# A gated causal convolution on one core: the last octet's second gate, transposes and output projection in a finer order, and the second window's remainder loaded ahead of its x

## The chip, the cores and the metric

The kernel runs on one core of one Trainium2 chip. The metric is device time in microseconds (us), from one launch of the whole program. A time is a median over several runs; the profile is of one further execution, whose own time differs a little from the median.

## The reference

`x` is 2 x 16000 x 144, `w` 15 x 144 x 288, `w_o` 144 x 144, all bfloat16. A causal convolution in time with 15 taps, two steps apart, gives 288 channels. The first 144 go through tanh, the other 144 through a sigmoid, the product `z` is multiplied by `w_o`.

```python
dil = 2
pad = (K - 1) * dil
xp = jnp.pad(x, ((0, 0), (pad, 0), (0, 0)))
h = sum(einsum('btc,cd->btd', xp[:, pad - i*dil : pad - i*dil + T, :], w[i]) for i in range(K))
z = jnp.tanh(h[..., :D]) * sigmoid(h[..., D:])
return z @ w_o
```

(The loop over the taps is written as a sum here; D is 144, K 15, T 16000.)

## The kernel before

**Windows and octets.** Each batch's 16000 time steps are cut into 8 windows of 2048 (the last overlaps its neighbour), so there are NW = 16. Within a window, time is 16 m + r: m runs over the 128 partitions of a result, r over 16 residues. An octet is the 8 residues of one parity of one window, so there are NO = 32 octets, two to a window. An octet's result `y` is 128 x 8 x 288 in float32: 8 rows (residues) of 288 channels.

**The convolution.** `load` brings a window's first 128 channels in by a transposing DMA (`xn`, line 89), channels on partitions. Differences of shifted copies of it (`d2`, `d4`, `d8`, `d24`, ..., line 160, on VectorE, DVE below) feed a scheme that needs fewer matrix multiplications than taps times rows; all the convolution's matmuls are issued at line 302. Partial sums go from PSUM through ScalarE copies (ACT, lines 331, 335, 366) and DVE additions (lines 369, 387, 392); the last of these write the rows of `y`. Rows 0, 2, 4, 6 of `y` come from the leaf B, rows 1 and 5 from `yC2_0` and `yC2_1`, rows 3 and 7 from `yC3_0` and `yC3_1`, which are written last.

**The remainder.** The last 16 of the 144 channels take another way. `gather` loads them as `xt` (line 99: 104 x 22 runs of 16 values, 32 bytes each). ACT copies them in order of residue (`xs`, line 113), DVE takes differences (`xs`, line 117), `spread` writes both to DRAM (`xg`, line 123), and two more transposing DMAs read them back as `rx` and `re` (line 128). All of these but window 0's `xt` and spreads are issued from SyncE's queue (SP).

**The gate and the output.** For each octet `act` issues a tanh and a sigmoid (ACT, line 397) over four rows of `y`: `th0`, `sg0` for rows 0, 2, 4, 6 and `th1`, `sg1` for rows 1, 3, 5, 7. `mult` forms the product `z` (DVE, line 404). A transposing DMA turns `z` into `zt` (line 408), `outproj` multiplies by `w_o` in three groups of at most three rows (line 434), `project_out` copies each group from PSUM to the window's output tile `o` (line 424 on ACT, 426 on DVE), and `store` writes a window (line 450).

**The last octets.** Octet 31's `z` is laid out by row (`by_phase`): blocks 0 to 7 hold 128 channels of a row each, block 8 the 16 remaining channels of all rows. TensorE (PE) transposes it with an identity matrix (`z_by_pe`, line 418), four blocks to a PSUM bank, and `outproj` takes block 8 first (line 438, against `wo_bd`), then a block for each row (line 441, against `wo_m`). Octets 29, 30 and 31 have their output in `finish_early`, just before octet 31's second product, and `finish`, after it; the last store is issued in two parts, from SP and ACT.

**What sets the order.** Nothing is scheduled by the compiler: each engine runs its instructions in the order in which the program issues them. In the steady part that order is a hand-written list, `PLAN`, of names with the octet that they are early or late by; `first` is the order of the opening. `late2 = [(2, "xl")]` stands ahead of it, so that window 1's `xn` (octet 2 is its first) is issued right behind window 0's `rx` and `re`; window 1's `xt` follows from `PLAN`.

PSUM is in three pools: `ps_a` (2 banks, `bank(True)`), `ps_bc` (5 banks, `bank(False)`) and `ps_o` (1 bank). A new tile waits for the readers of the one whose bank it takes.

Of the kernel before, what the change touches and what calls it, by code (L numbers as in the profile page):

```python
# [8 lines left out]
BF16 = mybir.dt.bfloat16  # L9
# [17 lines left out]
def kernel(  # L27
# [146 lines left out]
    def bank(a):  # L174
        return ps_a.tile([P, 512], F32, name="a", tag="a") if a else ps_bc.tile([P, 512], F32, name="bc", tag="bc")
# [169 lines left out]
    class Octet:  # L345
# [45 lines left out]
            y = self.get(y_pool, "y", [P, 8, D2], F32)  # L391
            nc.vector.tensor_tensor(out=y[:, k + 4 * i, :], in0=self.t[q][:, i, :], in1=ts[i][:, 0:D2], op=op)  # L392

        def act(self, k, name, lo, func):
            t = act_pool.tile([P, 4, D], BF16, name=name)
            self.g[name, k] = t
            nc.scalar.activation(out=t[:], in_=self.t["y"][:, k::2, lo:lo + D], func=func)  # L397

        def mult(self, k, part):
            z = self.get(z_pool, "z", [P, 9, CM], BF16)  # L400
            o, lo, n = dict(a=(z[:, k:8:2, :], 0, CM), b=(z[:, 8, :].rearrange("p (r c) -> p r c", c=CR)[:, k::2, :], CM, CR),
                            z=(z[:].rearrange("p g c -> p (g c)").rearrange("p (r c) -> p r c", c=D)[:, k::2, :], 0, D))[part]
            th, sg = self.g["th", k], self.g["sg", k]
            nc.vector.tensor_tensor(out=o, in0=th[:, :, lo:lo + n], in1=sg[:, :, lo:lo + n], op=ALU.mult)  # L404

    def z_load(z):
        zt = zt_pool.tile([P, 9, P], BF16, name="zt")
# [3 lines left out]
    def z_by_pe(o, blocks, by):  # L411

        zt, z = o.get(zt_pool, "zt", [P, 9, P], BF16), o.t["z"]
        for i in range(0, len(blocks), 4):
            b = blocks[i:i + 4]
            ps = bank(True)[:].bitcast(BF16).rearrange("p (g m) -> p g m", m=256)
            for k, g in enumerate(b):
                nc.tensor.transpose(ps[:, k, 0:P], z[:, g, :], ident[:])
            copy_by(by, zt[:, b[0]:b[-1] + 1:2, :], ps[:, 0:len(b), 0:P])
        o.zt = zt  # L420

    def copy_by(by, o, a):
        if by == "ACT":
            nc.scalar.copy(out=o, in_=a)  # L424
        else:
            nc.vector.tensor_copy(out=o, in_=a)  # L426

    def outproj(o, g, end=False):
        r0, n = 3 * g, min(3, 8 - 3 * g)
        o.po[g] = bank(False) if end else ps_o.tile([P, 512], F32, name="po", tag="po")  # L430
        if not o.by_phase:
            for c in range(r0, r0 + n + 1):
                a, e = max(c - 1, r0), min(c + 1, r0 + n)
                nc.tensor.matmul(o.po[g][:, (a - r0) * D:(e - r0) * D], lhsT=o.zt[:, c, :],  # L434
                                 rhs=wo_z[:, c, a - c + 1:e - c + 1, :].rearrange("p r e -> p (r e)"), start=c == r0, stop=c == r0 + n,
                                 skip_group_check=True)
            return
        nc.tensor.matmul(o.po[g][:, 0:n * D], lhsT=o.zt[:, 8, :], rhs=wo_bd[:, r0:r0 + n, :].rearrange("p r e -> p (r e)"),  # L438
                         start=True, stop=False)
        for i in range(n):  # L440
            nc.tensor.matmul(o.po[g][:, i * D:(i + 1) * D], lhsT=o.zt[:, r0 + i, :], rhs=wo_m[:], start=False, stop=i == n - 1)  # L441

    def project_out(o, ob, g, by="ACT"):
        r0, n = 3 * g, min(3, 8 - 3 * g)
# [13 lines left out]
    def issue(n, name):  # L458
        wi, rho = octs[n]
        if name == "xl":  # L460
            sets[wi].update(load(wi))
            sets[wi].update(steps=derive_steps(sets[wi]))
            return
        s = sets[wi]
        if name in fetch:
            fetch[name](wi)
            return
        if name in s["steps"]:
            s["steps"][name]()
            return  # L470
        if n not in live:
            live[n] = Octet(s, rho)
            live[n].by_phase = n == NO - 1
        o = live[n]
        if name[0] in "vkpd" and name[1] in "ABCE":
            leaf = getattr(o, name[1:3] if name[1] == "A" else name[1] + "1")
            if name[0] == "v":
                leaf.common()
            elif name[0] == "k":
                leaf.copy()  # L480
            else:
                (leaf.private if name[0] == "p" else leaf.dup)(int(name[-1]))
        elif name[:2] == "t3":
            o.t3(int(name[-1]))
        elif name[:3] == "a1s":
            o.a1s(int(name[-1]))
        elif name[0] == "q":
            o.q(*((o.A2, "q2") if name[1] == "2" else (o.A3, "q3")), int(name[-1]),
                ALU.subtract if name[1] == "2" else ALU.add)
        elif name[0] in "BC":  # L490
            getattr(o, name[0:2])(int(name[-1]))
        elif name[0] == "y":
            leaf = {"B": o.B1, "C": o.C1, "E": o.E1}["E" if name[1:3] == "C3" else name[1]]
            ts, q = (leaf.other, "q3") if name[1:3] == "B3" else (leaf.ts, "t3" if name[1:3] == "C3" else "q2")
            k = (0 if name[1] == "B" else 1) + (2 if name[2] == "3" else 0)
            o.out_y(k, ts, q, ALU.subtract if name[1] == "B" else ALU.add, int(name[-1]))
        elif name[:2] == "th":
            o.act(int(name[2]), "th", 0, ACT.Tanh)
        elif name[:2] == "sg":
            o.act(int(name[2]), "sg", D, ACT.Sigmoid)  # L500
        elif name[0] == "m":
            for part in "ab" if o.by_phase else "z":
                o.mult(int(name[1]), part)
        elif name == "zt":
            o.zt = z_load(o.t["z"])
        elif name[0] == "g":
            outproj(o, int(name[1]))
        elif name[:2] == "po":
            project_out(o, window_out(n), int(name[2]))
        else:  # L510
            assert name == "ost"
            store(wi, nc.scalar)

    def window_out(n):
        wi = octs[n][0]
        if wi not in outs:
            outs[wi] = os_pool.tile([P, 16, D], BF16, name="o")
        return outs[wi]

    def finish_early():  # L520

        n = NO - 3
        for g in range(3):
            outproj(live[n], g, g > 0)
        for g, by in ((0, "DVE"), (1, "DVE"), (2, "ACT")):
            project_out(live[n], window_out(n), g, by)
        z_by_pe(live[NO - 1], [0, 2, 4, 6], "ACT")

    def finish():
        n = NO - 2  # L530
        store(NW - 2, nc.sync)
        for g in range(3):
            outproj(live[n], g, True)
        for g in (0, 1):
            project_out(live[n], window_out(n), g)
        z_by_pe(live[n + 1], [1, 3, 5, 7], "DVE")
        z_by_pe(live[n + 1], [8], "DVE")
        project_out(live[n], outs[NW - 1], 2, "DVE")
        for g in range(3):
            outproj(live[n + 1], g, True)  # L540
        for g, by in ((0, "ACT"), (1, "DVE"), (2, "ACT")):
            project_out(live[n + 1], outs[NW - 1], g, by)
        store(NW - 1, nc.sync, 0, P // 2)
        store(NW - 1, nc.scalar, P // 2)

# [1 line left out]
    even = set(pre0) | set(fetch) | {"xl"}  # L547
    outwards = {"g0", "g1", "g2", "po0", "po1", "po2", "ost"}
    at_wg = next((at, i) for i, (name, at) in enumerate(plan) if name == "wg")
    def weights_out():  # L550

        nc.gpsimd.memset(wo_z[:], 0.0)
        nc.gpsimd.memset(wo_bd[:], 0.0)
        held = const.tile([1, 1], BF16)
        nc.gpsimd.tensor_copy(out=held[:], in_=ev[0:1, 0, 0:1])
        for g in range(9):
            if g:
                nc.gpsimd.dma_start(out=wo_z[0:CR * g, g, 0, :], in_=w_o[D - CR * g:D, :])
            if g < 8:
                nc.gpsimd.dma_start(out=wo_z[CR * g:P, g, 1, :], in_=w_o[0:P - CR * g, :])  # L560
        nc.gpsimd.dma_start(out=wo_m[:], in_=w_o[0:CM, :])
        for g in range(NG):
            nc.gpsimd.dma_start(out=wo_bd[g * CR:(g + 1) * CR, g, :], in_=w_o[CM:D, :])

    def evs():
# [3 lines left out]
    first = ["vA1", "kA1", lambda: raw_sums(1, (0,)), lambda: keep(1), "pA1_0", "pA1_1", "a1s_0", "a1s_1", "vA2", "kA2", lambda: keep(2), "vB",  # L569
             "kB", "pA2_0", "q2_0", "pA2_1", "q2_1", "vA3", "kA3", "pB_0", "dB_0", "pB_1", "dB_1", lambda: pre0["d24"](slice(1, 2)), "pA3_0",  # L570
             "q3_0", "pA3_1", "B2_0", "q3_1", "B2_1", evs, "yB2_0", pre0["d248"]]
    late2 = [(2, "xl")]
    for n, name in late2:
        issue(n, name)
    for f in first:
# [3 lines left out]
                  (n + at, n > 1 and n + at < 0, i, n, name) for i, (name, at) in enumerate(plan) for n in range(NO)  # L579
                  if not (name in even and (n % 2 or n == 0) or name == "ost" and n % 2 == 0  # L580
                          or name in outwards and n >= NO - 3 or name == "zt" and n == NO - 1))
    gates = [(NO - 1, "m1")]
    for *_, n, name in todo:
        if (n, name) in done:
            continue
        if (n, name) in gates:
            gates.clear()
            finish_early()
        issue(n, name)
    finish()  # L590
# [1 line left out]
_INS = ['x', 'w', 'w_o']  # L592
_OUTS = [((2, 16000, 144), 'bfloat16')]
# [25 lines left out]
```

## Time and profile before

| | us |
|---|---|
| median of 3 runs | 332.19 (331.83 to 332.69) |
| profiled execution, its own time | 332.82 |
| its span, first to last instruction | 330.8 |
| PE busy | 321.4 (97%) |
| PE's weight loads busy | 303.1 (92%) |
| DVE busy | 293.5 (89%) |
| ACT busy | 242.0 (73%) |
| POOL busy | 26.3 (8%) |

The span is what lies between the first and the last instruction; the time of the execution holds some 2 us more. PE is busy nearly all through, with a mean granted clock of 0.999. The opening (to about 24 us) and the end (from about 321 us) are the stretches in which PE waits for others.

In the profile's rows a start and a duration are in us from the span's start. "xn<-in_x_dram" is a write of tile xn from the input. "[0.66 <-DVE y L392]" behind a row says that the engine had been idle for 0.66 us and that a write of y on DVE, line 392, ended it. SPq and ACTq are the times that the queues took to issue a DMA, not the transfers.

### The profile page before, as it was taken

The numbers are of one execution on the slowest core, as the hardware profiler recorded it, in microseconds if no ns is written. First come the engines' busy times: TensorE is split into PE (matmuls) and PEld (weight loads), VectorE is DVE, ScalarE is ACT, GpSimd is POOL, SyncE is SP. The second block draws the span as 40 slices with busy tenths as digits, with TensorE's granted clock in tenths as the row PEclk, the third lists the DMA queues.
The fourth block names the chain that finished last, engine by engine and source line by source line (L and its number), as shares of the span: only waits on it lengthen the run. The fifth ranks groups of instructions, "written<-read, shape, count | busy, mean of one in ns | idle before, by whom it ended". The sixth has DMA issues, their size and how long they took to land.

```text
span 330.8 us, 7432 instructions
## 1 busy us (share of the span) xinstructions
PE 321.4 (97%) x2657; PEld 303.1 (92%) x2657; DVE 293.5 (89%) x664; ACT 242.0 (73%) x571; POOL 26.3 (8%) x56
## 2 busy tenths in 40 slices
PE   8899999999999999999999999999999999999993
PEld 3589999999999999999999999999999999999982
DVE  2889999989999998999999899999989999998683
ACT  2737777777877777788777778877777787777763
POOL 5959100000000000000000000000000000000000
PEclk9999999999999999999999999999999999999999
DMA  8779897895949579594979769495986859594113
GB/s 173 160 139 157 155 210 138 151 185 100 206 109 204 151 130 222 77 213 102 175 181 169 157 119 187 109 209 137 145 208 119 171 112 189 154 143 132 38 36 129
DMA packets 194993, 49.64 MB, mean 150 GB/s; under 512 B 190487, under 2 KB 192896, under 8 KB 194957
## 3 DMA queue, kind: packets, MB, share of 16 engines
q1 hardware_dynamic: 188894, 40.07, 69.6%
q10 hardware_dynamic: 4799, 8.58, 7.0%
q0 software_dynamic: 1264, 0.53, 0.9%
q8 instruction: 20, 0.33, 0.4%
q14 instruction: 16, 0.13, 0.1%
HBM read 2.82 MB, written 11.40 MB: 43 GB/s over the span
## 4 chain that ended last, share of the span: by engine, by line
PE 90%; DMA 4%; SPq 2%; DVE 2%; issue 1%; POOL 1%; ACT 0%; DVEq 0%
PE bc L302 56%; PE a L302 25%; PE po L434 9%; DMA xn<-in_x_dram 2%; DMA xt<-in_x_dram 1%; SPq L128 1%; DMA xg<-zero 1%; SPq L89 1%; DVE d L160 0%; DVE o L426 0%; DVE y L392 0%; DVE z L404 0%; POOL xg L123 0%; PE bc L438 0%; PE bc L441 0%
## 5 line engine op out<-in xcount | busy, mean ns | idle before, releaser
L302 PEld LDWEIGHTS <-d 128*128 128x128 bf16 x1792 | 225.4, 145 | 7.8 <-issue 1.4
L302 PE MATMUL bc<-w_all,d 128*128 128x288 bf16 x832 | 140.0, 286 | 0.3 <-DVE t L387 0.3
L392 DVE TENSOR_TENSOR y<-q,bc 128x288 f32<-128x288 f32 x192 | 86.4, 450 | 7.6 <-PE bc L302 5.7
L331 ACT COPY bc<-bc 128x288 f32<-128x288 f32 x97 | 38.5, 397 | 30.1 <-PE bc L302 24.3
L369 DVE TENSOR_TENSOR q<-a1s,a 128x288 f32<-128x288 f32 x126 | 54.2, 451 | 1.5 <-PE a L302 0.8
L424 ACT CAST o<-po 128x432 bf16<-128x432 f32 (+1 forms) x87 | 41.7, 479 | 17.1 <-PE po L434 17.1
L160 DVE TENSOR_TENSOR d<-d 128x516 bf16<-128x516 bf16 (+3 forms) x65 | 52.2, 805 | 0.0
L302 PE MATMUL a<-sm,d 128*128 128x288 bf16 x252 | 50.2, 286 | 0.0
L331 ACT COPY a<-a 128x288 f32<-128x288 f32 x95 | 36.6, 386 | 13.6 <-PE a L302 10.6
L160 DVE TENSOR_TENSOR d<-xn 128x516 bf16<-128x516 bf16 (+2 forms) x48 | 41.1, 859 | 5.1 <-DMA xn<-in_x_dram 5.1
L397 ACT ACTIVATE th<-y 128x576 bf16<-128x576 f32 x64 | 43.9, 685 | 1.1 <-DVE y L392 1.1
L397 ACT ACTIVATE sg<-y 128x576 bf16<-128x576 f32 x64 | 43.7, 683 | 0.0
L434 PE MATMUL po<-wo_z,zt 128*128 128x144 bf16 (+1 forms) x323 | 43.4, 253 | 0.0
L302 PE MATMUL bc<-bc,d 128*128 128x288 bf16 x256 | 41.8, 286 | 0.0
L302 PE MATMUL bc<-wo_p,re 128*128 128x288 bf16 x128 | 36.6, 286 | 0.0
L302 PE MATMUL bc<-we_r,re 128*128 128x288 bf16 x128 | 36.6, 286 | 0.0
L387 DVE TENSOR_TENSOR t<-q,bc 128x288 f32<-128x288 f32 x64 | 28.8, 451 | 8.3 <-PE bc L302 8.3
L434 PEld LDWEIGHTS <-zt 128*128 128x128 bf16 x341 | 29.9, 98 | 4.1
L335 ACT COPY bc<-bc 128x288 f32<-128x288 f32 x64 | 25.0, 393 | 11.2 <-PE bc L302 7.0
L392 DVE TENSOR_TENSOR y<-t,bc 128x288 f32<-128x288 f32 x64 | 26.1, 450 | 5.9 <-PE bc L302 5.9
L404 DVE TENSOR_TENSOR z<-th,sg 128x576 bf16<-128x576 bf16 (+1 forms) x66 | 29.1, 443 | 0.0
L302 PEld LDWEIGHTS <-re 128*128 128x128 bf16 x256 | 28.8, 113 | 0.0
(79 smaller groups left out, 275.5 us busy)
## 6 DMA issues: line engine op xcount, KB each, us to landing
out_dram<-o ACTq DMA_DIRECT2D x13, 576.0 KB
xg<-xs SPq DMA_DIRECT2D x30, 65.0 KB
xt<-in_x_dram SPq DMA_DIRECT2D x13, 71.5 KB
w_all<-in_w_dram SPq DMA_DIRECT2D x3, 288.0 KB
out_dram<-o SPq DMA_DIRECT2D x1, 576.0 KB
zt<-z SPq DMA_TRANSPOSE x31
out_dram<-o ACTq DMA_DIRECT2D x1, 468.0 KB
out_dram<-o ACTq DMA_DIRECT2D x1, 288.0 KB
```

Of the source, the lines that this page charges most:

```text
L89: nc.sync.dma_start_transpose(out=xn[:, lo:WB], in_=src)
L160: nc.vector.tensor_tensor(out=o, in0=a, in1=b_, op=ALU.subtract)
L302: nc.tensor.matmul(ps[:, 0:D2], lhsT=l, rhs=r, start=start, stop=stop, skip_group_check=on)
L331: nc.scalar.copy(out=self.ts[1][:, 0:D2], in_=self.ts[0][:, 0:D2])
L335: nc.scalar.copy(out=self.other[i][:, 0:D2], in_=self.ts[i][:, 0:D2])
L369: nc.vector.tensor_tensor(out=self.get(cp_pool, name, [P, 2, D2], F32)[:, i, :], in0=self.t["a1s"][:, i, :], in1=leaf.ts[i][:, 0:D2], op=op)
L387: nc.vector.tensor_tensor(out=self.get(cp_pool, "t3", [P, 2, D2], F32)[:, i, :], in0=self.t["q3"][:, i, :], in1=self.C1.ts[i][:, 0:D2], op ...
L392: nc.vector.tensor_tensor(out=y[:, k + 4 * i, :], in0=self.t[q][:, i, :], in1=ts[i][:, 0:D2], op=op)
L397: nc.scalar.activation(out=t[:], in_=self.t["y"][:, k::2, lo:lo + D], func=func)
L404: nc.vector.tensor_tensor(out=o, in0=th[:, :, lo:lo + n], in1=sg[:, :, lo:lo + n], op=ALU.mult)
L424: nc.scalar.copy(out=o, in_=a)
L434: nc.tensor.matmul(o.po[g][:, (a - r0) * D:(e - r0) * D], lhsT=o.zt[:, c, :], rhs=wo_z[:, c, a - c + 1:e - c + 1, :].rearrange("p r e -> p ...
```

## The change

Two things are changed.

**At the opening**, `late2` holds window 1's `xt` ahead of its `xn`: on SP's queue the DMA of line 99 comes before that of line 89, and nothing else stands between them. What DVE and ACT run, and in which order, is as before.

**At the end**, for octet 31:

- The second gate is cut in two. `act(1, 4)` takes rows 1 and 5, `act(3, 4)` rows 3 and 7, each with a tanh and a sigmoid of 128 x 288; the product follows for each half (a part of 128 x 256 for the blocks, one of 128 x 32 for block 8).
- The transposes go by blocks 0, 2, 4, 6, then 1, 5, then 3, 7, 8; `zt` holds them in that order (`o.at`). The copies out of PSUM are: ACT for the first two, DVE for the third.
- `outproj_last` issues the projections by block, in the order 0, 2, 4, 1, 5, 6, 8 (row group 0), 3, 9 (block 8 for group 1), 7, 10 (block 8 for group 2). Block 8 now comes last within each group of rows, and group 0 takes the bank of `ps_o`.
- Octet 30's projection is spread: its first group goes ahead of octet 31's first transposes, the other two behind them.
- Octet 29's copies to the output are ACT, DVE, DVE (before: DVE, DVE, ACT) and stand behind all of octet 31's gate and products, as do octet 30's (DVE, ACT, ACT; before: ACT, ACT, DVE). The store of the window before the last is behind octet 29's.

```diff
-        def act(self, k, name, lo, func):
-            t = act_pool.tile([P, 4, D], BF16, name=name)
-            self.g[name, k] = t
-            nc.scalar.activation(out=t[:], in_=self.t["y"][:, k::2, lo:lo + D], func=func)
+        def act(self, k, step=2):
+            for name, lo, func in (("th", 0, ACT.Tanh), ("sg", D, ACT.Sigmoid)):
+                self.gate(k, name, lo, func, step)
+
+        def gate(self, k, name, lo, func, step=2):
+            t = self.g[name, k] = act_pool.tile([P, 8 // step, D], BF16, name=name + "h" * (step == 4))
+            nc.scalar.activation(out=t[:], in_=self.t["y"][:, k::step, lo:lo + D], func=func)
...
     def z_by_pe(o, blocks, by):
         zt, z = o.get(zt_pool, "zt", [P, 9, P], BF16), o.t["z"]
-        for i in range(0, len(blocks), 4):
-            b = blocks[i:i + 4]
-            ps = bank(True)[:].bitcast(BF16).rearrange("p (g m) -> p g m", m=256)
-            for k, g in enumerate(b):
-                nc.tensor.transpose(ps[:, k, 0:P], z[:, g, :], ident[:])
-            copy_by(by, zt[:, b[0]:b[-1] + 1:2, :], ps[:, 0:len(b), 0:P])
-        o.zt = zt
+        ps = bank(True)[:].bitcast(BF16).rearrange("p (g m) -> p g m", m=256)
+        n = len(o.at)
+        for k, g in enumerate(blocks):
+            o.at[g] = n + k
+            nc.tensor.transpose(ps[:, k, 0:P], z[:, g, :], ident[:])
+        copy_by(by, zt[:, n:n + len(blocks), :], ps[:, 0:len(blocks), 0:P])
...
+    def outproj_last(o, blocks):
+        for c in blocks:
+            g, lo, n, w_ = (c // 3, c % 3, 1, wo_m[:]) if c < 8 else \
+                (c - 8, 0, min(3, 8 - 3 * (c - 8)), wo_bd[:, 3 * c - 24:min(3 * c - 21, 8), :].rearrange("p r e -> p (r e)"))
+            new = g not in o.po
+            if new:
+                o.po[g] = bank(False) if g else ps_o.tile([P, 512], F32, name="po", tag="po")
+            nc.tensor.matmul(o.po[g][:, lo * D:(lo + n) * D], lhsT=o.t["zt"][:, o.at[min(c, 8)], :], rhs=w_, start=new, stop=c >= 8,
+                             skip_group_check=True)
...
     def finish():
+        a, b, c = (live[n] for n in range(NO - 3, NO))
+        c.at = {}
+        window_out(NO - 1)
+        for g in range(3):
+            outproj(a, g, g > 0)
+        outproj(b, 0, True)
+        z_by_pe(c, [0, 2, 4, 6], "ACT")
+        c.mult(1, 4)
+        c.mult(3, 4)
+        for g, by in ((0, "ACT"), (1, "DVE"), (2, "DVE")):
+            project_out(a, outs[NW - 2], g, by)
+        store(NW - 2, nc.sync)
+        for g in (1, 2):
+            outproj(b, g, True)
+        z_by_pe(c, [1, 5], "ACT")
+        z_by_pe(c, [3, 7, 8], "DVE")
+        for g, by in ((0, "DVE"), (1, "ACT"), (2, "ACT")):
+            project_out(b, outs[NW - 1], g, by)
+        outproj_last(c, [0, 2, 4, 1, 5, 6, 8, 3, 9, 7, 10])
+        for g, by in ((0, "ACT"), (1, "DVE"), (2, "ACT")):
+            project_out(c, outs[NW - 1], g, by)
         store(NW - 1, nc.sync, 0, P // 2)
         store(NW - 1, nc.scalar, P // 2)
...
-    late2 = [(2, "xl")]
+    late2 = [(2, "xt"), (2, "xl")]
...
-    gates = [(NO - 1, "m1")]
+    last = {"th1": lambda: live[NO - 1].act(1, 4), "sg1": lambda: live[NO - 1].act(3, 4), "m1": finish}
     for *_, n, name in todo:
         if (n, name) in done:
             continue
-        if (n, name) in gates:
-            gates.clear()
-            finish_early()
-        issue(n, name)
-    finish()
+        if n == NO - 1 and name in last:
+            last[name]()
+        else:
+            issue(n, name)
```

More of the change, by code (lines that the diff above doesn't have):

```diff
@@ L392, in out_y, with mult @@
             nc.vector.tensor_tensor(out=y[:, k + 4 * i, :], in0=self.t[q][:, i, :], in1=ts[i][:, 0:D2], op=op)
-        def act(self, k, name, lo, func):
-            t = act_pool.tile([P, 4, D], BF16, name=name)
-            self.g[name, k] = t
-            nc.scalar.activation(out=t[:], in_=self.t["y"][:, k::2, lo:lo + D], func=func)
-        def mult(self, k, part):
+        def act(self, k, step=2):
[4 more added lines that the diff above has]
+            nc.scalar.activation(out=t[:], in_=self.t["y"][:, k::step, lo:lo + D], func=func)
+        def mult(self, k, step=2):
             z = self.get(z_pool, "z", [P, 9, CM], BF16)
-            o, lo, n = dict(a=(z[:, k:8:2, :], 0, CM), b=(z[:, 8, :].rearrange("p (r c) -> p r c", c=CR)[:, k::2, :], CM, CR),
-                            z=(z[:].rearrange("p g c -> p (g c)").rearrange("p (r c) -> p r c", c=D)[:, k::2, :], 0, D))[part]
             th, sg = self.g["th", k], self.g["sg", k]
-            nc.vector.tensor_tensor(out=o, in0=th[:, :, lo:lo + n], in1=sg[:, :, lo:lo + n], op=ALU.mult)
+            if not self.by_phase:
+                parts = [(z[:].rearrange("p g c -> p (g c)").rearrange("p (r c) -> p r c", c=D)[:, k::step, :], 0, D)]
+            else:
+                parts = [(z[:, k:8:step, :], 0, CM), (z[:, 8, :].rearrange("p (r c) -> p r c", c=CR)[:, k::step, :], CM, CR)]
+            for o, lo, n in parts:
+                nc.vector.tensor_tensor(out=o, in0=th[:, :, lo:lo + n], in1=sg[:, :, lo:lo + n], op=ALU.mult)
     def z_load(z):
@@ L430, in outproj @@
         o.po[g] = bank(False) if end else ps_o.tile([P, 512], F32, name="po", tag="po")
[L431 to L441, printed above, removed]
+        for c in range(r0, r0 + n + 1):
+            a, e = max(c - 1, r0), min(c + 1, r0 + n)
+            nc.tensor.matmul(o.po[g][:, (a - r0) * D:(e - r0) * D], lhsT=o.zt[:, c, :],
+                             rhs=wo_z[:, c, a - c + 1:e - c + 1, :].rearrange("p r e -> p (r e)"), start=c == r0, stop=c == r0 + n,
+                             skip_group_check=True)
[7 more added lines that the diff above has]
+            nc.tensor.matmul(o.po[g][:, lo * D:(lo + n) * D], lhsT=o.t["zt"][:, o.at[min(c, 8)], :], rhs=w_, start=new, stop=c >= 8,
+                             skip_group_check=True)
     def project_out(o, ob, g, by="ACT"):
@@ L497, in issue @@
         elif name[:2] == "th":
-            o.act(int(name[2]), "th", 0, ACT.Tanh)
+            o.gate(int(name[2]), "th", 0, ACT.Tanh)
         elif name[:2] == "sg":
-            o.act(int(name[2]), "sg", D, ACT.Sigmoid)
+            o.gate(int(name[2]), "sg", D, ACT.Sigmoid)
         elif name[0] == "m":
-            for part in "ab" if o.by_phase else "z":
-                o.mult(int(name[1]), part)
+            o.mult(int(name[1]))
         elif name == "zt":
@@ L518, in window_out, with finish @@
         return outs[wi]
-    def finish_early():
-        n = NO - 3
+    def finish():
+        a, b, c = (live[n] for n in range(NO - 3, NO))
+        c.at = {}
+        window_out(NO - 1)
         for g in range(3):
[L524 to L530, printed above, removed]
-        store(NW - 2, nc.sync)
[L532 to L540, printed above, removed]
+            outproj(a, g, g > 0)
[5 more added lines that the diff above has]
+            project_out(a, outs[NW - 2], g, by)
+        store(NW - 2, nc.sync)
+        for g in (1, 2):
[5 more added lines that the diff above has]
+        outproj_last(c, [0, 2, 4, 1, 5, 6, 8, 3, 9, 7, 10])
         for g, by in ((0, "ACT"), (1, "DVE"), (2, "ACT")):
-            project_out(live[n + 1], outs[NW - 1], g, by)
+            project_out(c, outs[NW - 1], g, by)
         store(NW - 1, nc.sync, 0, P // 2)
@@ L585 @@
             continue
-        if (n, name) in gates:
-            gates.clear()
-            finish_early()
-        issue(n, name)
-    finish()
+        if n == NO - 1 and name in last:
+            last[name]()
+        else:
+            issue(n, name)
 _INS = ['x', 'w', 'w_o']
```

## The prediction

> **What bounds the kernel now.** I read the chain of waits first, then who ended PE's idle time, then the opening and the end instruction by instruction. The chain's shares by engine, and all of PE's waits between 20 and 320 us:
>
> ```profile
> PE 90%; DMA 4%; SPq 2%; DVE 2%; issue 1%; POOL 1%; ACT 0%; DVEq 0%
> ...
> PE bc L302 <- DVE y L392: 0.7, 1, 0.7
> PE bc L302 <- DVE t L387: 0.3, 1, 0.3
> ```
>
> PE is the bound: one wait of 0.7 at the opening, one of 0.3 near 318.7, none between. So whatever moves PE's start at the opening moves everything behind it by as much, and at the end only the path to the last store counts. Both parts of the change lie in those stretches. The opening, as PE, DVE and SP's queue had it:
>
> ```profile
> 22.51 0.41 PE L302 MATMUL a<-av,d 128*128 128x288 bf16 x2
> 23.58 0.41 PE L302 MATMUL bc<-ev,d 128*128 128x288 bf16 x2 [0.66 <-DVE y L392]
> ...
> 20.12 0.65 DVE L160 TENSOR_TENSOR d<-d 128x516 bf16<-128x516 bf16 x1
> 20.73 1.24 DVE L160 TENSOR_TENSOR d<-xn 128x2078 bf16<-128x2078 bf16 x1
> 22.84 0.32 DVE L117 TENSOR_TENSOR xs<-xt 104x320 bf16<-104x320 bf16 x1 [0.86 <-DMA xt<-in_x_dram]
> 23.08 0.45 DVE L392 TENSOR_TENSOR y<-q,bc 128x288 f32<-128x288 f32 x1
> ...
> 16.30 2.07 SPq L89 DMA_TRANSPOSE xn<-in_x_dram  x1
> 18.41 0.56 SPq L99 DMA_DIRECT2D xt<-in_x_dram  x1
> ```
>
> The order on DVE is the point: d2 of window 1 (from `xn`), the remainder's difference (from `xt`), then the `y` that PE wants. d2 started as soon as its predecessor was done, so `xn` had landed by 20.73. `xt`, issued behind it, was released at 22.82 by the chain, and DVE sat idle 0.86 for it. That `y` released PE after 0.66 of idleness. How the transfers shared the DMA engines, from 17 to 23 us in slices of 0.15 us (busy tenths, then GB/s):
>
> ```profile
> DMA  9999987999999999999966999996111591110009
> GB/s 288 288 292 290 219 151 138 217 254 263 254 275 288 294 288 290 288 292 231 133 43 38 57 167 53 63 56 35 9 3 3 67 159 21 20 18 14 0 0 188
> ```
>
> `re`, to the dip near 17.8, and `xn`, to about 19.8, run near 290 GB/s; then `xt`'s 32-byte runs crawl at some 55 GB/s to about 21.05, and a thin remainder trickles to 22.5. The slice of 167 GB/s is one 16 KB instruction fetch (0.9% of 16 engines over 6 us, 0.86 us on one engine): it holds up that engine's share.
>
> The end, ACT and then DVE:
>
> ```profile
> 320.45 0.67 ACT L397 ACTIVATE sg<-y 128x576 bf16<-128x576 f32 x1
> 321.91 0.68 ACT L397 ACTIVATE th<-y 128x576 bf16<-128x576 f32 x1 [0.80 <-DVE y L392]
> 322.50 0.67 ACT L397 ACTIVATE sg<-y 128x576 bf16<-128x576 f32 x1
> ...
> 325.31 1.02 ACT L424 CAST o<-bc 128x432 bf16<-128x432 f32 x2 [0.53 <-PE bc L441]
> ...
> 321.00 0.82 DVE L392 TENSOR_TENSOR y<-t,bc 128x288 f32<-128x288 f32 x2 [0.28 <-PE bc L302]
> 321.73 0.52 DVE L404 TENSOR_TENSOR z<-th,sg 128x512 bf16<-128x512 bf16 x2
> 322.17 0.60 DVE L426 CAST o<-po 128x432 bf16<-128x432 f32 x1
> ...
> 323.20 0.53 DVE L404 TENSOR_TENSOR z<-th,sg 128x512 bf16<-128x512 bf16 x2
> 324.12 0.56 DVE L426 COPY zt<-a 128x512 bf16<-128x512 bf16 x2 [0.39 <-PE a L418]
> 325.68 0.61 DVE L426 CAST o<-bc 128x432 bf16<-128x432 f32 x1 [0.64 <-PE bc L441]
> ```
>
> ACT waits 0.80 for the last rows of `y` with half of what the gate needs (rows 1 and 5) already there at 320.72. From there the path is serial: gate to 323.17, product to 323.73, transposes, copies to 324.68, eleven matmuls to 325.89, copies to 326.33, stores.
>
> **The opening, step by step.** SP issues `xt` at 16.30 in place of `xn`, and `xn` 0.56 later; nothing else is moved past. `xt` is then no longer late: its bulk takes about 1.35 us (19.7 to 21.05 above), so it follows `re` from about 17.8 and is there long before DVE asks. But `xn` now stands behind it, and what waits for `xn` is longer: d2 comes first on DVE, and behind d2 are queued the difference, the `y`, and PE. Call X the time at which `xn` lands. From X: d2 1.20 (1.24, the next starting 0.04 before its end, as after 20.12), the difference 0.24 (22.84 to 23.08), then `y`. So `y` starts at X + 0.02 + 1.20 + 0.24 = X + 1.46, against 23.08: PE moves by X - 21.62.
>
> X from below: 20.73 plus `xt`'s bulk of 1.35 gives 22.08, a loss of 0.46. From above: the same three transfers and the same fetch go through the same engines, and the last piece of the pair landed at 22.82; with 0.2 for the later write behind it, 23.0, a loss of 1.38. I take the nearer row, 22.82: the held-up engine has the same sum of work in either order, and then it is `xn` that ends on it. Loss 1.20 us, which PE, without idle time further on, carries to the end. The spreads and window 1's `rx`, `re` cost nothing: the first spread leaves earlier (ACT's copy no longer waits 0.46), the second when the difference is done, near 24.4, so that `rx` is issued near 25.4, where it was at 25.67. If that cover failed, a first use near 33.4 leaves over 3 us more.
>
> Here a rule of the Trainium skill speaks ("DMA: Bandwidth & Descriptors", section "Queues, rings and completion order"): on each DMA engine a queue's descriptors are consumed in ring order. The slices agree, `xt`'s slow runs starting as `xn`'s fast ones end. By it X is 22.08 or later, never 20.73.
>
> **The end, step by step**, on the old clock. The rows 1 and 5 are there at 320.72, ACT is free at 321.04. An ACTIVATE of 128 x 288 is not in this stretch; at line 237 it takes 0.41, and starts follow 0.08 before an end. First half 321.04 to 321.79, hidden in the old idle 0.80. Second half after `y` (321.82 + 0.09): 321.91 to 322.65, where it was 323.17. The halves cost 4 x 0.41 against 2 x 0.68, all of the surplus inside the idle time.
>
> DVE: products of 128 x 256 and 128 x 32, by a line through 128 x 512 (0.42) and 128 x 64 (0.185), are 0.29 and 0.17; the last end at 323.07 (before 323.73). Then octet 29's two copies, moved behind them, 0.60 and 0.45, with overlaps to 323.96: these are the price of putting the gate first. PE's last transposes wait for z at 323.07 and for ACT to empty their bank (322.66 to 323.25) and end near 323.65, so DVE's copy of blocks 3, 7, 8 starts at 323.88 and ends at 324.23 (0.35, between 0.425 for 512 and 0.215 for 128). On ACT the copy of blocks 0 to 6 (0.59), octet 29's group 0 (0.52), the copy of 1, 5 (0.37) and octet 30's two groups (0.53, 0.40) fill 322.66 to 324.70.
>
> PE has done six of the eleven projections by then; five are left after 324.28: block 8 (spacing 0.18), 3 (0.06), 9 (0.18), 7 (0.06), 10. Group 0 is complete at 324.64, group 1 at 324.9, the last at 325.06 (before 325.89). Last copies: ACT 324.72 to 325.24 and to 325.56, DVE 324.93 to 325.54. Stores at 325.58 instead of 326.35: gain 0.77. The store of the window before goes out near 324.1 instead of 323.48; in the DMA view of the end its data were moved by 325.8, 2.3 us after its issue, so near 326.4 now, when the last store's begin to move (0.65 us after issue); they meet hardly at all. From below 0.45 (each of four cross-engine hops 0.08 worse), from above 0.9. I take 0.75.
>
> **Sum.** +1.20 - 0.75 = +0.45 on the profiled execution: span 330.8 to 331.25, its time 332.82 to 333.27. That execution stood 0.63 above the median; on the median 332.19 + 0.45 = 332.6.
>
> **The rivals.** *xn is not held back* (it lands by 21): then `y` is ready before PE is, all 0.66 of PE's wait goes, and the sum is -0.66 - 0.75: 330.8. For it: `xt` is small, 71.5 KB. Against it: the slices, in which those 71.5 KB occupy the engines for 1.35 us. The same page, section "Anatomy of one DMA", prices movement at bytes / 436 GB/s; by that `xt` would hold `xn` back by an estimated 0.17 us and this rival would be right. The slices contradict it for 32-byte runs.
>
> *xn lands later still*: POOL's weight loads (67 and 159 GB/s in the slices near 21.7) now fall on `xn`'s tail instead of `xt`'s. With X = 23.6 the opening loses 1.98 and the time is 332.19 + 1.98 - 0.75 = 333.4. It decides from X = 23.4. For it: three such loads stand in the window; against it: 23.6 is 0.6 beyond the bound above.
>
> *The clock slows*: PE now idles near 1.9 us at a stretch (0.66 + 1.20). The first warm-up matmuls of 128 x 512 stand 0.43 apart up to about 5.4 us and 0.215 after, so 4.2 us at half speed, if it came back, would cost 2.1: 334.7. Nothing slows after the two idle 0.66 in this trace, which is all it can say. The Trainium skill ("TensorE: Matmul & The Clock Gate", the rules at its end) sets the limit near 3 us of idleness; by that this rival fails.
>
> *The end gives nothing*: the later store of the window before, or a copy mis-ordered, takes the 0.75 back; 332.19 + 1.20 = 333.4.
>
> **How the numbers follow.** Forecast 0.57, xn not held back 0.16, xn later still 0.12, clock 0.06, end gives nothing 0.09. This kernel's measurement tells about 0.3%, 1.0 us, from no change: the forecast lies within it, the first rival is faster by more, the last three slower by more. So faster 0.16, same 0.57, slower 0.27. The forecast's own range is 332.19 + 0.46 - 0.9 to 332.19 + 1.38 - 0.45, or 331.8 to 333.1; to hold 8 in 10 it reaches to the first rival and to the two at 333.4: 330.8 to 333.6.
>
> **What would show it.** Right: DVE idle before d2 with `xn` as releaser, ending between 22.1 and 23.0; no wait for `xt`; PE's idle near 23 at 1.1 to 2.0 us; from the last row of `y` to the final store's issue 0.7 to 0.8 us less. Wrong: d2 starting at 20.7 again, or PE's wait gone (first rival); matmul spacing doubled after the gap (clock); ACT or DVE waiting for a bank between 322 and 325 (the end).

## The result and the profile after

The changed kernel takes 335.05 us (median of 10 runs, 333.57 to 336.95) against 332.45 for the kernel before (10 runs, 331.83 to 333.39): a ratio of 1.0081, 95% interval [1.0053, 1.0108]. It is slower by about 2.6 us, outside the range of 330.8 to 333.6 that was given, and its runs scatter more than twice as widely as before. Its profiled execution was its fastest run: 333.57, with a span of 331.7 against 330.8.

The chain's shares and PE's waits (line; total, times, longest in us) of the profiled execution:

```profile
PE 90%; DMA 5%; DVE 1%; SPq 1%; issue 1%; POOL 1%; ACT 0%; DVEq 0%
...
PE bc L302 <- DVE y L392: 2.7, 1, 2.7
PE bc L302 <- DVE t L387: 0.3, 1, 0.3
```

It is the same place and the same `y` as before, but PE waits 2.7 us for it instead of 0.7. The opening on PE, DVE and SP's queue:

```profile
22.11 0.41 PE L302 MATMUL a<-av,d 128*128 128x288 bf16 x2
25.24 0.41 PE L302 MATMUL bc<-ev,d 128*128 128x288 bf16 x2 [2.72 <-DVE y L392]
...
19.72 0.66 DVE L160 TENSOR_TENSOR d<-d 128x516 bf16<-128x516 bf16 x1
23.34 1.24 DVE L160 TENSOR_TENSOR d<-xn 128x2078 bf16<-128x2078 bf16 x1 [2.97 <-DMA xn<-in_x_dram]
24.50 0.32 DVE L117 TENSOR_TENSOR xs<-xt 104x320 bf16<-104x320 bf16 x1
24.74 0.45 DVE L392 TENSOR_TENSOR y<-q,bc 128x288 f32<-128x288 f32 x1
...
15.85 0.56 SPq L99 DMA_DIRECT2D xt<-in_x_dram  x1
16.45 3.32 SPq L89 DMA_TRANSPOSE xn<-in_x_dram  x1
```

Nobody waits for `xt` any more (the `xs` row has no idle time before it). DVE now sits idle 2.97 us for `xn`, does d2, and comes to `y` 1.66 later than before (24.74 against 23.08). The whole opening stands 0.40 earlier in this execution (PE's last matmuls ahead of the wait start at 22.11 against 22.51), so against PE's own work `y` is 2.06 later, which is what the wait grew by. `xn` landed near 23.3; the prediction had taken 22.8 and had allowed 23.0. The transfers from 17 to 23 us in slices of 0.15 us (busy tenths, GB/s) show why:

```profile
DMA  9999848999721024799999900010000799999991
GB/s 282 232 102 61 49 26 47 56 60 67 43 16 8 0 31 102 172 266 396 273 266 229 24 0 0 0 9 9 9 10 9 160 282 295 287 290 294 385 356 24
```

`xt`'s 32-byte runs go from 17.3 to about 18.7. `xn` begins at 19.1, runs for a little over 1 us, and stops: from 20.3 to 21.65 there is next to nothing (9 GB/s, a trickle), then the rest of `xn` follows at 290 GB/s. The window holds one 16 KB instruction fetch, as before, but here it falls in `xn`. In slices of 0.0625 us from 19.5 it is the one of 545 GB/s, at 19.81, half a microsecond ahead of the stop:

```profile
GB/s 217 274 279 258 287 545 270 283 270 274 274 225 168 33 0 0 0 0 0 0 0 0 4 8 8 8 12 8 8 8 8 12 8 12 12 143 287 279 283 303
...
q8 instruction: 1, 0.02, 2.7%
```

Its 2.7% of 16 engines over 2.5 us are 1.1 us on one engine.

The end, ACT and DVE (thh and sgh are the halves of the second gate):

```profile
322.70 0.43 ACT L401 ACTIVATE thh<-y 128x288 bf16<-128x288 f32 x1
323.52 0.44 ACT L401 ACTIVATE thh<-y 128x288 bf16<-128x288 f32 x1
323.88 0.43 ACT L401 ACTIVATE sgh<-y 128x288 bf16<-128x288 f32 x1
...
327.24 0.55 ACTq L461 DMA_DIRECT2D out_dram<-o  x1
...
322.67 0.82 DVE L392 TENSOR_TENSOR y<-t,bc 128x288 f32<-128x288 f32 x2 [0.28 <-PE bc L302]
323.85 0.86 DVE L411 TENSOR_TENSOR z<-thh,sgh 128x256 bf16<-128x256 bf16 x4
324.63 0.97 DVE L432 CAST o<-bc 128x432 bf16<-128x432 f32 x2
325.51 0.35 DVE L432 COPY zt<-a 128x384 bf16<-128x384 bf16 x1
326.56 0.61 DVE L432 CAST o<-bc 128x432 bf16<-128x432 f32 x1 [0.18 <-PE bc L451]
```

From the last row of `y` (322.67 + 0.82 = 323.49) to ACT's part of the last store it takes 3.75, where it took 4.55 (321.82 to 326.37). The end gains 0.80.

So the profiled execution lost 1.66 in the opening and gained 0.80 at the end, which is its 0.9 us of span. The median lies 1.5 us above this execution's own time, and that part is not in this profile. The experiments look for it.

### The profile page after: what moved, and what is told of

Same layout as the page of the kernel before. It is cut to its first block, busy times and chain, and to the rows that moved or that the text cites. A ratio compares the mean times of both kernels' runs of the same rounds, so it can differ in the third digit from the quotient of the medians.

```text
span 331.7 us, 7433 instructions
## 1 busy us (share of the span) xinstructions
PE 321.9 (97%) x2657; PEld 303.4 (91%) x2657; DVE 293.3 (88%) x665; ACT 242.3 (73%) x574; POOL 26.4 (8%) x56
## 4 chain that ended last, share of the span: by engine, by line
PE 90%; DMA 5%; DVE 1%; SPq 1%; issue 1%; POOL 1%; ACT 0%; DVEq 0%
PE bc L302 56%; PE a L302 25%; PE po L439 9%; DMA xn<-in_x_dram 4%; SPq L128 1%; DMA xg<-zero 1%; DVE d L160 0%; DVE y L392 0%; POOL xg L123 0%; PE po L451 0%; DVE o L432 0%; ACT zt L430 0%; SPq L99 0%; DVE xs L117 0%; POOL xg L213 0%
## 5 line engine op out<-in xcount | busy, mean ns | idle before, releaser
L430 ACT CAST o<-po 128x432 bf16<-128x432 f32 (+1 forms) x89 | 42.8, 480 | 17.1 <-PE po L439 17.1
L401 ACT ACTIVATE th<-y 128x576 bf16<-128x576 f32 x63 | 43.2, 685 | 0.3 <-DVE y L392 0.3
L387 DVE TENSOR_TENSOR t<-q,bc 128x288 f32<-128x288 f32 x64 | 28.9, 451 | 8.3 <-PE bc L302 8.3
```

Source lines behind the costliest of these rows:

```text
L387: nc.vector.tensor_tensor(out=self.get(cp_pool, "t3", [P, 2, D2], F32)[:, i, :], in0=self.t["q3"][:, i, :], in1=self.C1.ts[i][:, 0:D2], op ...
L401: nc.scalar.activation(out=t[:], in_=self.t["y"][:, k::step, lo:lo + D], func=func)
```

## The experiments

The ratios are against runs of the kernel before on the same chip, with 95% intervals; "over" and "below" are medians against these. A ratio lies near that of the means, so a few high or low runs move it more than they move the medians.

**Each part alone.** The end alone (the opening's list put back):

```diff
-    late2 = [(2, "xt"), (2, "xl")]
+    late2 = [(2, "xl")]
```

> The changed end with the opening of before. Theory A (all of the loss is in the opening: xn lands late, PE idles some 2.7 us, and in most runs its clock is then lowered for a while): about 0.75 us faster than before, PE's wait near 23 us 0.7 again, mean granted clock 0.998 or more in every run and no more scatter than before. Rival B (the end costs time in the median runs, which the one profile does not show): not faster than before, or slower by up to 1.5 us, with the scatter of the changed kernel (3.4 us from lowest to highest).

It took 331.44, 0.88 below: 0.9983 [0.9973, 0.9994], with 0.9 us from lowest to highest; by the ratio it is 0.6 below (0.2 to 0.9). Both hold the 0.80 of the profile, and B falls. The mean granted clock, expected at 0.998 or more in every run, was 0.994 to 1.000. That is no sign of a wait: the kernel before has 0.994 to 0.999 in its runs, and in e1_end_only's profile the clock is below 1.00 only behind 326 us, where PE has nothing left to do. So below, the spans and the clock stretch by stretch decide.

The opening alone (the kernel before with the changed list):

> The changed opening (xt ahead of xn on SP's queue) with the end of before. Theory A: about 3.3 us slower than before in the median (2.6 of the changed kernel and the 0.75 that its end gives), d2 on DVE idle for some 3 us until xn lands near 23.3, PE's wait 2.7, granted clock between 0.985 and 0.997 with a scatter of some 3 us. Rival B: 1.2 to 1.7 us slower and no scatter.

It took 335.58 (334.88 to 337.09), 3.3 over: 1.0113 [1.0091, 1.0134]. The scatter of 2.2 is less than the 3 expected. All of the loss, and more, is in this one line. And its profile caught what the changed kernel's had not. Stretches of 3.4 us around PE's wait (length; busy time and instructions of PE, weight loads, DVE, ACT, POOL; granted clock; DMA share, GB/s):

```profile
core 0: us, PE busy (x) PEld busy (x) DVE busy (x) ACT busy (x) POOL busy (x), PEclk, DMA share, GB/s
22.80:26.20 3.40, 0.60 (x5) 0.43 (x4) 2.42 (x5) 0.58 (x2) 3.40 (x7) 1.00 0.44 91
26.20:29.70 3.50, 3.50 (x17) 2.42 (x16) 3.14 (x8) 0.38 (x1) 3.50 (x8) 0.51 1.00 92
29.70:33.10 3.40, 3.40 (x30) 3.34 (x28) 3.06 (x8) 2.45 (x6) 2.67 (x6) 1.00 1.12 220
```

Behind PE's wait of 2.8 us comes a stretch at a granted clock of 0.5 in which PE is busy throughout and gets 17 matmuls done, where the next stretch holds 30. Thirteen matmuls at 0.122 us apiece (four take 0.49 at the full clock) are 1.6 us. On the profile's page this is a single 7 among the nines of the clock's digits, in slices of 8 us, and a mean clock of 0.994 as some runs of the kernel before have it too.

**Is it the clock, or does xn's landing scatter?** The changed kernel with PE kept at work through the wait:

```diff
     for *_, n, name in todo:
         if (n, name) in done:
             continue
+        if (n, name) == (0, "vE"):
+            keep(12)
```

> The changed kernel with twelve matmuls of 128 x 512 on zeros (2.6 us) put on PE just where it waits for y in the opening. Theory A (the clock is lowered because PE idles 2.7 us): every run at a granted clock of 0.998 or more, scatter as before, and the median at what the changed kernel's profiled run had, about 0.9 us over before (333.2 to 333.6). Rival C (it is the landing of xn that scatters, up to 3 us later from run to run; the clock is a by-product): median near 335 still, scatter 3 us.

It took 333.41, all seven runs within 0.6 us: 1.0039 [1.0024, 1.0054] (eleven of the twelve matmuls are in the trace):

```profile
22.36 2.75 PE L288 MATMUL po<-zero 128*128 128x512 bf16 x11
25.20 0.41 PE L302 MATMUL bc<-ev,d 128*128 128x288 bf16 x2
```

PE's real work resumes at 25.20, as late as in the changed kernel (25.24), since `xn` landed no earlier. Yet the scatter and some 1.5 us of the median are gone (1.09 over, for 2.60). The mean clock missed what was expected here too (0.995 to 0.999, for 0.998 or more), but the spans, 331.2 to 331.8, hold no slow stretch. C falls: what scatters is the clock.

**Idleness alone, with no transfer moved.** The kernel before with DVE held up just ahead of that `y`; the width is 1720, 980 and, in a later run, 2060:

```diff
+        if (n, name) == (0, "yB2_1"):
+            for _ in range(2):
+                nc.vector.tensor_tensor(out=idle[:, 0:1720], in0=sets[0]["x"][:, 0:1720], in1=sets[0]["x"][:, 0:1720], op=ALU.subtract)
```

> The kernel before, with two DVE subtractions (128 x 1720 each, about 2.05 us together, result unused) put just ahead of the y that releases PE in the opening: PE idles 2.7 us there, and no DMA is moved. Theory A: 2.05 us from the delay and 1 to 1.7 us more from the clock, so about 3.3 us slower than before, with a clock of 0.985 to 0.997 and a scatter of some 3 us. Rival C: 2.05 us slower, clock 0.998 or more, no more scatter than before.

> As e4_gap27 with two subtractions of 128 x 980, some 1.2 us together, so that PE idles about 1.8 us in the opening, which is what the prediction expected of the change. Theory A (the clock falls only when idleness fills most of a 3.4 us record): 1.2 us slower than before, clock 1.0 around the gap, no run that stands out. Rival (any gap well over 0.7 us lowers it): some of the runs 1 to 2 us slower still.

> As e4_gap27 with two subtractions of 128 x 2060, 2.45 us together: PE idles 2.7 to 3.0 us in the opening, no transfer is moved. Theory A: 2.45 us of delay (less 0.2 where y was not late) and in most runs 1 to 1.7 more for a stretch of lowered clock: median 3.0 to 4.0 over before, scatter 2 to 3 us. Rival C (idleness alone does not lower it): 2.2 to 2.5 over before, no scatter.

| run | PE's wait in the profile | time | over | ratio |
|---|---|---|---|---|
| e4_gap19 | 1.6 | 333.08 (332.29 to 334.5) | 0.97 | 1.0033 [1.0019, 1.0047] |
| e4_gap27 | 2.3 | 334.06 (333.57 to 336.69) | 1.74 | 1.0077 [1.0047, 1.0108] |
| e14_gap30 | 2.6 | 335.56 (334.56 to 336.26) | 3.35 | 1.0097 [1.0075, 1.0119] |

In spans, e4_gap19 costs what its delay adds (1.6 - 0.7 = 0.9): all twelve lie between 330.3 and 331.6, and its two slowest runs, 334.13 and 334.5, stand out by time that lies outside the span (3.0 and 2.9 us of it, for 1.7 to 2.5 in the others). e4_gap27 missed what theory A expected: its median is 1.74 over, near the 1.6 that its wait grew by, and one run of six, with a span 1.9 above the median one and a clock of 0.993, points to a slow stretch (the other high one, 335.5, is at 0.998, with 3.0 us outside its span). e14_gap30 adds 1.9 of waiting and costs 3.35; four of its six runs have spans of 333.3 to 334.3 at 0.989 to 0.994, the other two 331.9 and 332.8 at 0.998. Its profile has the same stretch behind the wait, at a granted clock of 0.50 and with 17 matmuls (columns as above):

```profile
26.30:29.70 3.40, 3.40 (x17) 2.33 (x15) 3.11 (x9) 0.38 (x1) 3.40 (x7) 0.50 1.00 218
```

So a wait of PE lowers the clock by itself, with no transfer moved: by the spans in none of twelve runs at 1.6 us, one of six at 2.3 and most at 2.6. The waits came out shorter than the labels say because `xt` landed earlier in these runs.

**Why xn is so late.** The fetch comes when PE has run through some 200 instructions (matmuls and weight loads: 197 by 20.5 us in the kernel before, 195 by 17.15 in e11_after_fetch_40, 193 by 11.0 in e13_after_fetch_full). Cutting the warm-up matmuls into more and narrower ones moves it without moving PE's work.

```diff
-    NWARM = 20
+    NWARM = 80
...
-        nc.tensor.matmul(t[:], lhsT=zero[:, 0:P], rhs=zero[:], start=True, stop=True)
+        nc.tensor.matmul(t[:, 0:P], lhsT=zero[:, 0:P], rhs=zero[:, 0:P], start=True, stop=True)
```

> The changed kernel with its twenty warm-up matmuls of 128 x 512 cut into eighty of 128 x 128: the same PE time, 120 more PE instructions, so that the first 16 KB instruction fetch (at 19.8 to 21.1 us so far, in the middle of xn's transfer) comes near 11 us, when little moves. Theory D (the fetch holds up one DMA engine, and with it the whole transposing DMA): the hole in xn's transfer goes, xn lands near 21.8 to 22.3 instead of 23.3 to 23.8, PE's wait is 1.2 to 1.6 instead of 2.7, its clock stays up, and the time is 0 to 0.6 us over before. Rival E (the hole comes from the queue's own descriptors behind the 32-byte runs): xn lands at 23.3 or later still and the time stays near 335.

It took 332.03: 0.9991 [0.9980, 1.0003], 3 us below the changed kernel. d2 started at 21.63 and PE waited 1.1. D holds, E falls. (In this run and in e8 to e11 the last warm-up matmul of a bank covers only a part of its columns, and as far as the code tells this changes what octet 0 accumulates onto in the rest. What is issued, and when, is not touched, so these five runs serve for their times alone; e12 and e13 below do without that.) The next four vary that, with warm-ups that go over all columns of a bank in turn:

> The changed kernel with the fetch moved as in e8_end_fetch (e5_fetch_earlier again, with warm-ups that go over all columns of the banks). Theory D: xn lands at 21.5 to 22.0, PE's wait is 1.0 to 1.3, clock up, time near that of e5_fetch_earlier (332.0), 3 us below the changed kernel. Otherwise 333 or more.

331.89, 0.9996 [0.9988, 1.0005]; d2 at 21.82, PE's wait 1.1.

> The changed kernel with forty warm-up matmuls of 128 x 256, so 40 more PE instructions: the first fetch comes near 17.5 us, in xt's transfer or at its end, and not in xn's. Theory D (a fetch during xn stops all of xn; one during xt only makes one engine late): xn lands at 22.0 to 22.8, PE's wait 1.4 to 2.2, time 332.3 to 333.2. If the place of the fetch did not matter between the two: xn at 23.3, time 335.

333.20 (331.59 to 334.26), 1.0030 [1.0012, 1.0047]; d2 at 22.46, PE's wait 2.0. The fetch was at 17.15. The slices (17 to 23 us) and d2:

```profile
DMA  9999998896310000003479999999999991071111
GB/s 269 247 61 64 53 55 46 45 57 31 17 7 5 6 5 5 0 0 39 99 164 280 282 287 294 287 294 288 288 294 290 295 330 16 2 134 54 27 23 39
...
22.46 1.24 DVE L160 TENSOR_TENSOR d<-xn 128x2078 bf16<-128x2078 bf16 x1 [2.24 <-DMA xn<-in_x_dram]
```

Here `xn` runs in one piece, but only from 19.7: it does not begin on the free engines while the held-up one works off its share of `xt` (the 5 to 7 GB/s until 19.4). In that profile a wait of 2.0 sufficed for the clock: 0.51 from 25.5 to 28.9, 16 matmuls. It and one more of the ten runs have a mean clock of 0.990.

The kernel before, and its opening with the changed end, with the fetch moved:

> The kernel before with the fetch moved alone. Theory D: PE's wait of 0.7 near 23 us goes, time 0.5 to 0.7 below before (331.4 to 331.7). Rival (the fetch costs nothing where xt comes last): 0 to 0.2 below.

> The changed end, the loads in the order of before, and the first instruction fetch moved to near 10.5 us (eighty warm-up matmuls of 128 x 128, over all columns of their banks). Theory D (the fetch also held up the last of xt in the kernel before): xt lands near 21.9 instead of 22.8, y starts near 22.2, PE's wait near 23 us is gone, and the time is 0.8 + 0.5 to 0.7 below before: 330.7 to 331.0, under e1_end_only. Rival (other waits take its place, as in e6 and e7): 331.4 to 331.6, no better than e1_end_only.

331.64, 0.9985 [0.9975, 0.9995], and 330.96, 0.9964 [0.9952, 0.9975]. In neither does PE wait for that `y`, though of the 0.66 only 0.47 shows in the medians of the first. So in the kernel before, too, the 0.66 was the fetch's doing: it had held up the last engine's piece of `xt`.

Last, the same with seven matmuls of 128 x 512, one to a bank, at the end of the warm-up:

```diff
-    NWARM = 20
+    NWARM = 79
...
-        nc.tensor.matmul(t[:], lhsT=zero[:, 0:P], rhs=zero[:], start=True, stop=True)
+        w_ = 64 if i < NWARM - 7 else 512
+        nc.tensor.matmul(t[:, 0:w_], lhsT=zero[:, 0:P], rhs=zero[:, 0:w_], start=True, stop=True)
```

> e9_after_fetch with the same warm-ups as e12_end_fetch_full. Theory D: xn lands near 21.8, PE's wait 1.0 to 1.3, time 331.7 to 332.3, some 3 us below the changed kernel. Rival: 333 or more.

The changed kernel with it: 332.00, 0.9995 [0.9981, 1.0008].

```profile
DMA  9999999999950335999999999999218201100720
GB/s 287 294 231 80 57 60 63 59 64 59 44 30 1 27 63 111 230 276 283 288 283 259 280 276 290 290 290 238 55 24 154 46 15 29 18 0 0 161 54 0
...
21.90 1.24 DVE L160 TENSOR_TENSOR d<-xn 128x2078 bf16<-128x2078 bf16 x1 [1.39 <-DMA xn<-in_x_dram]
```

No fetch in the window, no hole: `xn` from 19.1 to 21.2 in one piece, landed by 21.9. What is left is what the order alone costs: 1.3 us against e12_end_fetch_full, which has the same warm-ups and the old order.

> e8_end_fetch with seventy-two narrow warm-up matmuls (128 x 64) and then seven of 128 x 512, one for each bank: 118 more PE instructions than before, first fetch near 11 us. Theory D: xt lands near 21.9 or earlier, no wait of PE near 23 us, 1.0 to 1.5 us below before (330.6 to 331.1). Rival (the narrow warm-ups of e8_end_fetch made the gain): 331.4 or more, as e1_end_only.

330.71, 0.9950 [0.9930, 0.9969]: the fastest of all, 1.5 us below the kernel before. On DVE nothing waits:

```profile
20.67 1.24 DVE L160 TENSOR_TENSOR d<-xn 128x2078 bf16<-128x2078 bf16 x1
21.88 0.33 DVE L117 TENSOR_TENSOR xs<-xt 104x320 bf16<-104x320 bf16 x1
22.12 0.45 DVE L393 TENSOR_TENSOR y<-q,bc 128x288 f32<-128x288 f32 x1
```

**Taking y out from behind the loads.** Two more orders of DVE's work for window 1: `moved` gives some steps another place in the list (`at` holds the places).

```diff
+    at = {name: i for i, (name, _) in enumerate(plan)}
+    moved = dict(cr=at["t3_1"] + .3, dr=at["t3_1"] + .4, wg=at["t3_1"] + .5, d2=at["yB3_1"] + .5, d4=at["q2_1"] + .5)
-    todo = sorted((2 + at_wg[0], False, at_wg[1] - .5, n, name) if n == 2 and name in ("cr", "dr") else
+    todo = sorted((1, False, moved[name], n, name) if n == 2 and name in moved else
```

> The changed kernel with window 1's d2 and d4 moved on DVE behind the four y and t3 of the opening that PE waits for, and the remainder's xs copies ahead of the last of these y: same loads, same transfers, xn still lands late. Theory A (xn's lateness costs only because d2 stands ahead of y): PE's wait near 23 us gone or below 0.4, clock 1.0, time 0.7 to 1.5 us below before (331.0 to 331.7). Rival (the transfers themselves disturb PE or what follows): still over before.

> The changed end, the loads in the order of before, and only the remainder's xs copies (ACT and DVE) moved behind the y and t3 of the opening: xn lands near 20.7 as before, d2 follows at once, and y no longer stands behind xs, which waits for xt. Expected: PE's wait of 0.7 gone, so 0.75 + 0.5 to 0.66 below before, 330.9 to 331.3. If the wait only moves to the next t3 or y, no better than e1_end_only.

e6_y_first took 331.92, 0.9996 [0.9986, 1.0006]; e7_xs_behind_t3 (loads in the old order, without `d2` and `d4` in `moved`) 331.63, 0.9981 [0.9968, 0.9993]. PE's waits from 14 to 40 us in the one and in the other:

```profile
PE bc L302 <- DMA rx<-xg: 0.5, 1, 0.5
PE a L302 <- DVE q L369: 0.4, 1, 0.4
PE bc L302 <- ACT bc L335: 0.3, 1, 0.3
```

```profile
PE po L439 <- DMA zt<-z: 0.5, 1, 0.5
PE bc L302 <- DMA rx<-xg: 0.4, 1, 0.4
```

In both PE no longer waits for that `y`. In e6 it runs as soon as its predecessor is done, while `xn` is still on its way (at some 290 GB/s until 20.9):

```profile
20.36 0.48 DVE L392 TENSOR_TENSOR y<-q,bc 128x288 f32<-128x288 f32 x1
```

So it never needed `xn`: what made it late in the changed kernel was its place behind d2. (The transfers of e6 were not those of the changed kernel, as had been expected: its fetch came at 20.75, near the end of `xn`, and there is no hole.) But the gain expected did not come in full. e6's interval holds 1, where 0.7 to 1.5 us were expected, and e7 is no better than e1_end_only. New waits took part of it, 0.7 for `q` and a copy in the one, 0.5 for a `zt` in the other; where the rest of e6's gain went stays open.

## Why the prediction was wrong

- *The end* was right: 0.75 foreseen, 0.80 in the profile, 0.88 in e1_end_only's medians and 0.6 by its ratio; the halves of the gate took 0.43 for 0.41, the copy of three blocks 0.35.
- *The queue's order* was right: `xt` no longer late, `xn` behind it, d2 and then `y` behind `xn`, with 1.40 from the start of d2 to that of `y` (23.34 to 24.74) for the 1.44 reckoned. e5, e9 and e13 show the order's own price: X near 21.6 to 21.9, a touch under the lower bound of 22.08, and a wait of 1.1.
- *X itself* is the first step that failed: "the held-up engine has the same sum of work in either order". That holds for one engine, not for the transfer. In the changed order all of `xn` stood still while one engine was held up (the hole at 20.3 to 21.65), where in the old order the other engines had gone on with `xt`. X was 23.34 for 22.82, and 1.66 were lost in the opening for 1.20. This term was mis-sized by 0.46, and by 0.86 against PE's own work, which was ahead by 0.40 (2.06 for 1.20; e2_opening_only, whose opening stands as in the kernel before, has `y` at 25.18, 2.10 later). That is about what the rival *xn lands later still* had reckoned with (1.98), but the weight loads that it named were not the cause: they are there in e13 too, and the hole is not. By itself this left the time within the range: e3_pe_kept_busy, with this landing and no slow stretch, took 333.41.
- *The clock* is the step that took it out of the range. It was a rival with a chance of 0.06, at 334.7, "PE now idles near 1.9 us at a stretch", and its only evidence from the trace was that nothing slows after idle stretches of 0.66, which says nothing on 2 us or more. It was priced at 2.1 us; it costs 1.6 when it strikes, in a stretch of 3.4 us as e2_opening_only shows, and it struck more often because the wait was 2.7 and not 1.9. That the rival's 334.7 lies so near the 335.05 measured is luck: its price for the clock was too high by about as much as its opening was too low.
- *The Trainium skill* was used for both. The ring order of the Trainium skill ("DMA: Bandwidth & Descriptors", "Queues, rings and completion order"), by which each DMA engine consumes a queue's descriptors in order, agrees with e13, where `xn` starts at 19.1 as `xt` ends. In e11 `xn` did not start on the free engines either, which an order on each engine alone does not ask for. The limit near 3 us in the Trainium skill ("TensorE: Matmul & The Clock Gate", the rules at its end) was what let the clock rival fall. Here the measurement decides otherwise, with the clock at 0.5 after waits of 2.0, 2.6 and 2.8 us. The same page of the Trainium skill says elsewhere (Part 1) that the gate looks at free-running windows of about 3.4 us; the stretches of 3.4 us agree with that, and so does a wait of 2.7 that in the changed kernel's own profile passed without it.
- Put together: 332.45 + 1.66 - 0.80 + about 1.6 in most runs gives 334.9, against 335.05 measured. (With 2.06 for the opening it is 335.3.)

What stays open is how much of a window a wait must fill, since the profile doesn't tell where it stood to the windows of most runs, and why a held-up engine stops the others in a transposing DMA.

## What to carry to other kernels

Before two loads on one queue are swapped, look at what stands behind each on the engine that consumes them: here the one with the longer work behind it had to land first, however late the other looked in the chain. Waits of PE of 2.0 to 2.8 us cost here, besides their length, some 1.6 us in part of the runs, for a stretch at half clock. A single profile may miss that, as the changed kernel's did; scatter in the runs, and spans that stand apart, are the sign to look for it. A wait in the opening may belong to an instruction fetch, which can be moved by changing the number of instructions ahead of it.

## What the runs showed of the hardware that was not expected

- One 16 KB instruction fetch, about 1 us on one of 16 DMA engines, stopped a transposing DMA on all of them for 1.35 us (20.3 to 21.65); in the profiles of e2_opening_only and e3_pe_kept_busy the same hole lasts from 21.2 to 22.7 and from 20.75 to 21.95. With the fetch out of the way d2 started 1.4 to 1.7 us earlier. A plain DMA with 32-byte runs went on on the other engines (some 55 GB/s behind the fetch in the kernel before).
- PE's granted clock fell to 0.5 for one stretch of 3.4 us after waits of 2.0 to 2.8 us, with 16 or 17 matmuls done where 30 are usual; after waits of 2.3 and 2.7 in two other profiles it did not.
- Moving one fetch, by cutting the warm-up matmuls, was worth 0.5 us in the kernel before (e10_before_fetch) and 0.6 with the changed end (1.50 below for 0.88, on two chips; the seventy-nine of e12 have 8192 columns in all for 10240, but PE then waits for its weights, 1.6 us for `w_all`).
